# Values of a chunked gated recurrence on all four quarters of the TensorE array: odd heads' scores moved to the other half of the partitions, odd heads of v loaded there too

## The chip, the cores and the metric

The kernel runs on one core of one Trainium2 chip. The metric is the device time of one execution in microseconds (us), the median of several runs. The profile's span is the stretch from the first to the last recorded instruction of one execution. It lies about 2 us below that execution's time.

The engines carry short names: PE is TensorE's matmul, PEld its weight load, DVE VectorE, ACT ScalarE, POOL GpSimd, SP SyncE. A "q" behind a name means that engine's issuing of DMAs. L641 is line 641 of the kernel's file. The change adds lines, so one piece of code has two numbers:

| code | before | after |
|---|---|---|
| transposes of f, k, q | L535 | L541 |
| carried part (kept x qh) | L609 | L615 |
| scores | L619 | L626 |
| values | L641 | L649 |
| new state | L667 | L674 |
| first, second layer of the MLP | L711, L718 | L718, L725 |

## The reference, cut to what matters

```python
# q, k, v, f_logit: (batch 4, heads 8, seq 768, head_dim 48), fp32
f = 1.0 / (1.0 + np.exp(-f_logit))
for t in range(S):
    state = f[:, :, t, :, None] * state + np.einsum('bhd,bhe->bhde', k[:, :, t], v[:, :, t])
    y[:, :, t] = np.einsum('bhd,bhde->bhe', q[:, :, t], state)
x = y.transpose(0, 2, 1, 3).reshape(B, S, H * D)       # (4, 768, 384)
xn = (x - mean) / np.sqrt(var + 1e-06) * g_ln
out = x + np.maximum(xn @ w_ch1, 0.0) @ w_ch2          # 384 -> 1536 -> 384
```

## The kernel before

The 768 steps are cut into 12 chunks of 64. Within a chunk the recurrence becomes four small products per pair of batch and head: the carried part (old state times scaled q), the scores (scaled k times scaled q, 64 x 64, with a causal mask), the values (masked scores times v) and the new state (k transposed times v). The MLP follows for the rows of the chunk. The order of all pieces of work is a hand-written plan: chunk n+1's small products are placed between pieces of chunk n's MLP.

The 128 partitions are used as two halves of 64. A batch `b` of a pair of batches owns half `b`, and `r` is 0 for even heads and 1 for odd ones. A small product uses one quarter of the array: a row half (the partitions that its operands lie on) and a column half (the output partitions). In the values both halves are `b`:

```python
ps = two_banks(f"ps{n}").rearrange("s r (e t) -> s r e t", t=T)
for e in range(GA):                                   # 8 pairs of heads
    for b in range(2):
        for r in range(2):
            seg = 2 * e + b
            nc.tensor.matmul(ps[half(b), r, e], lhsT=kh[head_rows(r), seg],
                             rhs=qh[head_rows(r), seg], start=True, stop=True)
# ... sc = ps * causal (VectorE), kt = transposes of kh ...
for across_ in range(2):
    for e, (g, a) in enumerate(pairs):
        for b in range(2):
            r = b ^ across_
            nc.tensor.matmul(py[half(b), r, e * D:(e + 1) * D],
                             lhsT=sc[half(b), r, e], rhs=vt[half(b), g, 2 * a + r],
                             start=n == 0 and e == 0, stop=True, skip_group_check=True)
# ... x copied from py (ScalarE), statistics; then the new state:
for e, (g, a) in enumerate(pairs):
    for r in range(2):
        for b in range(2):
            nc.tensor.matmul(pn[half(r), b, e * D:(e + 1) * D], lhsT=kt[half(b), e, half(r)],
                             rhs=vt[half(b), g, 2 * a + r], start=True, stop=True)
```

The start of the plan is listed piece by piece. In it `l1f` loads f of chunk 1, `f`, `r` and `w` fetch, convert and write a piece of the weights, `a1.values` is a stage of chunk 1 and `m0` a piece of chunk 0's MLP:

```python
START = """
l0v f l0k l0q f l1k l1f a0.gates l1q a0.after a0.k_across a0.upto
a0.k f a0.q a0.scores r a0.causal l1v w a0.kt a0.values r a0.stats
w a1.gates a0.state a0.norm a0.turn m0 r a1.after f a1.k_across f a1.upto
...
"""
```

One count needs care. The code has 32 matmuls of values per chunk (8 x 2 x 2), so 384 in 12 chunks, and the trace has 768 records of them. Each of these fp32 matmuls shows as two records. "64 matmuls" in the prediction and "x64" in the profile are records.

## Time and profile before

| what | before | how to read it |
|---|---|---|
| median of the 3 runs | 523.44 us | 522.62 to 523.45 |
| span of the profiled run | 521.5 us | |
| TensorE busy | 95% of the span | with the chain of waits, 90% of which is PE: TensorE sets the time |
| values, busy | 24.8 us in 768 records | 32 ns a record, where the other small products take 18 to 19 ns |
| one chunk in steady state | 40.48 us | from a carried part to that of the next chunk |

The prediction shows and reads the lines of this profile.

### The profile page before, as it was taken

The numbers are of one execution on the slowest core, as the hardware profiler recorded it, in microseconds if no ns is written. First come the engines' busy times: TensorE is split into PE (matmuls) and PEld (weight loads), VectorE is DVE, ScalarE is ACT, GpSimd is POOL, SyncE is SP. The second block draws the span as 40 slices with busy tenths as digits, with TensorE's granted clock in tenths as the row PEclk, the third lists the DMA queues.
The fourth block names the chain that finished last, engine by engine and source line by source line (L and its number), as shares of the span: only waits on it lengthen the run. The fifth ranks groups of instructions, "written<-read, shape, count | busy, mean of one in ns | idle before, by whom it ended". The sixth has DMA issues, their size and how long they took to land.

```text
span 521.5 us, 10893 instructions
## 1 busy us (share of the span) xinstructions
PE 495.8 (95%) x4841; PEld 380.1 (73%) x4841; DVE 201.0 (39%) x286; ACT 129.6 (25%) x255; POOL 41.4 (8%) x53
## 2 busy tenths in 40 slices
PE   2789897999999999999999999999999999999996
PEld 1668774668867867877876876876876876886773
DVE  6789557534323432431521612603512522522000
ACT  3457672002202112112112211211211211221210
POOL 3215235000000000000000000000000000000000
PEclk9979999999999999999999999999999999999999
DMA  9976565513303303402501601600700610000001
GB/s 170 177 206 218 118 160 76 108 31 69 69 16 65 74 4 63 87 3 51 102 3 36 116 3 25 127 3 16 132 6 16 118 20 16 17 1 16 17 1 35
DMA packets 109703, 33.83 MB, mean 65 GB/s; under 512 B 102736, under 2 KB 105808, under 8 KB 109648
## 3 DMA queue, kind: packets, MB, share of 16 engines
q1 hardware_dynamic: 108192, 32.85, 30.8%
q8 instruction: 40, 0.66, 0.5%
q10 hardware_dynamic: 1456, 0.20, 0.2%
q14 instruction: 15, 0.12, 0.1%
HBM read 28.31 MB, written 4.72 MB: 63 GB/s over the span
## 4 chain that ended last, share of the span: by engine, by line
PE 90%; DVE 4%; DMA 2%; ACT 1%; POOL 1%; issue 1%; ACTq 0%; SPq 0%; DVEq 0%; POOLq 0%
PE ph L711 35%; PE po L718 35%; PE tr L535 6%; PE py L641 5%; PE ps L619 2%; PE py L609 2%; PE kp L632 2%; PE pn L667 2%; PE xp L696 2%; DMA kraw<-in_k_dram 1%; DVE w_0body L507 1%; DMA fraw<-in_f_logit_dram 1%; POOL w L511 1%; DVE w_0body L504 1%; DVE w_0upper L509 1%
## 5 line engine op out<-in xcount | busy, mean ns | idle before, releaser
L718 PE MATMUL po<-w,h 128*128 128x384 f32 x576 | 195.2, 492 | 3.9 <-POOL w L511 3.9
L711 PE MATMUL ph<-xt,w 128*128 128x256 f32 x864 | 196.2, 383 | 0.5 <-ACT xt L698 0.5
L711 PEld LDWEIGHTS ph<-xt,w 128*128 128x128 f32 x864 | 163.2, 192 | 24.5 <-issue 0.9
L718 PEld LDWEIGHTS po<-w,h 128*128 128x128 f32 x576 | 107.3, 191 | 72.8 <-POOL w L511 5.1
L713 ACT ACTIVATE h<-ph 128x512 f32<-128x512 f32 x72 | 42.8, 596 | 167.0 <-PE ph L711 167.0
L723 DVE TENSOR_TENSOR o<-x,po 128x384 f32<-128x384 f32 x24 | 13.3, 554 | 117.4 <-PE po L718 117.4
L549 DVE TENSOR_TENSOR_SCAN after<-gates,ends 128x1040 f32<-128x1040 f32 (+1 forms) x13 | 28.0, 2155 | 34.9 <-ACT gates L568 34.9
L698 ACT ACTIVATE xt<-xp,gain 128x128 f32<-128x128 f32 x72 | 20.1, 373 | 84.7 <-PE xp L696 84.7
L656 DVE BATCH_NORM_STATS2 stats<-x 128x6 f32<-128x384 f32 x24 | 13.0, 543 | 67.7 <-ACT x L652 67.7
L623 DVE TENSOR_TENSOR sc<-ps,causal 128x1024 f32<-128x1024 f32 x12 | 14.7, 1225 | 53.3 <-PE ps L619 53.3
L658 POOL TENSOR_SCALAR rstd<-mv 128x2 f32<-128x2 f32 x12 | 2.8, 235 | 378.4 <-DVE mv L657 378.3
L561 DVE TENSOR_TENSOR_SCAN upto<-gates,starts 128x1040 f32<-128x1040 f32 (+1 forms) x13 | 28.1, 2158 | 0.5
L641 PEld LDWEIGHTS py<-v,sc 64*64 64x64 f32 x768 | 23.3, 135 | 6.6 <-issue 5.5
L652 ACT COPY x<-py 128x384 f32<-128x384 f32 x24 | 10.3, 481 | 64.0 <-PE py L641 64.0
L641 PE MATMUL py<-v,sc 64*64 64x48 f32 x768 | 24.8, 219 | 0.7 <-DVE sc L623 0.7
L634 ACT COPY kt<-kp 128x512 f32<-128x512 f32 x24 | 12.9, 589 | 46.2 <-PE kp L632 46.2
L587 DVE TENSOR_TENSOR qh<-tr,upto 128x512 f32<-128x512 f32 x24 | 15.6, 686 | 20.8 <-PE tr L535 20.8
L535 PE MATMUL tr<-ident,fraw 128*128 128x128 f32 x96 | 13.8, 286 | 6.1 <-POOL gates L445 4.6
L511 POOL TENSOR_TENSOR w<-w_0upper,w_0units 128x768 int32<-128x768 int32 x7 | 15.3, 2190 | 35.7 <-DVE w_0upper L509 35.7
L535 PE MATMUL tr<-ident,kraw 128*128 128x128 f32 x96 | 13.7, 288 | 4.7 <-DMA kraw<-in_k_dram 4.5
L535 PEld LDWEIGHTS tr<-ident,fraw 128*128 128x128 f32 x96 | 11.6, 148 | 7.9 <-POOL gates L445 4.6
L587 DVE TENSOR_TENSOR kh<-tr,after 128x512 f32<-128x512 f32 x24 | 15.3, 677 | 5.1 <-PE tr L535 5.1
(88 smaller groups left out, 307.0 us busy)
## 6 DMA issues: line engine op xcount, KB each, us to landing
w_0words<-in_moe_w_ch_dram SPq DMA_DIRECT2D x7, 768.0 KB, 5.0
v<-in_v_dram SPq DMA_DIRECT2D x48, 96.0 KB, 3.0
kraw<-in_k_dram SPq DMA_DIRECT2D x48, 96.0 KB, 3.1
qraw<-in_q_dram SPq DMA_DIRECT2D x48, 96.0 KB, 3.1
out_dram<-o SPq DMA_DIRECT2D x48, 96.0 KB, 2.2
fraw<-in_f_logit_dram SPq DMA_DIRECT2D x46, 96.0 KB, 3.1
w_256words<-in_moe_w_ch_dram SPq DMA_DIRECT2D x1, 768.0 KB, 5.7
w_512words<-in_moe_w_ch_dram SPq DMA_DIRECT2D x1, 768.0 KB, 6.9
```

The source lines that it names most:

```text
L511: nc.gpsimd.tensor_tensor(out=to.bitcast(I32), in0=upper, in1=units, op=ALU.add)
L535: nc.tensor.transpose(pt[:, a * P:(a + 1) * P], src[:, g, 2 * a:2 * a + 2].rearrange("p h e -> p (h e)"), ident)
L549: nc.vector.tensor_tensor_scan(out=after.rearrange(flat)[:, c0:c1][:, ::-1], data0=gt[:, c0 + 1:c1 + 1][:, ::-1], data1=ends.rearrange(fla ...
L561: nc.vector.tensor_tensor_scan(out=upto.rearrange(flat)[:, c0:c1], data0=gt[:, c0:c1], data1=st.rearrange(flat)[:, c0:c1], initial=0.0, op ...
L587: nc.vector.tensor_tensor(out=dst[:, segs], in0=pt, in1=by[:, segs, 1:E1], op=ALU.mult)
L623: nc.vector.tensor_tensor(out=sc.rearrange("s r e t -> s (r e) t"), in0=ps.rearrange("s r e t -> s (r e) t"), in1=causal.unsqueeze(1).broa ...
L641: nc.tensor.matmul(py[half(b), r, e * D:(e + 1) * D], lhsT=sc[half(b), r, e], rhs=vt[half(b), g, 2 * a + r], start=n == 0 and e == 0, stop ...
L698: nc.scalar.mul(out=xt[:, m, g * P:(g + 1) * P], in_=pt[:, m], mul=gain[:, m:m + 1])
L711: nc.tensor.matmul(ph[:, j], lhsT=w1[:, m, (i + j) * P:(i + j + 1) * P], rhs=xt[:, m], start=m == 0, stop=m == KD - 1)
L713: nc.scalar.activation(out=h[:, i:i + 2], in_=ph, func=AF.Relu)
L718: nc.tensor.matmul(po, lhsT=h[:, i, g * P:(g + 1) * P], rhs=w2[:, i], start=i == 0, stop=i == KF - 1)
L723: nc.vector.tensor_tensor(out=o, in0=x[:, g], in1=po, op=ALU.add)
```

## The change

Its intent is that the values use all four quarters of the array in place of two. Scores of an odd head are written to the other partition half, `b ^ r`. The values of that head then read their scores and their v there, so its v must also lie there: four extra DMAs per chunk load the odd heads of v into a tile `vx` with the two halves exchanged. Three buffers are made single along the way, to pay for `vx` in memory.

```diff
-l0v f l0k l0q f l1k l1f a0.gates l1q a0.after a0.k_across a0.upto
-a0.k f a0.q a0.scores r a0.causal l1v w a0.kt a0.values r a0.stats
+l0v f l0k l0q l0x f l1k l1f a0.gates l1q a0.after a0.k_across a0.upto
+a0.k f a0.q a0.scores r a0.causal l1v l1x w a0.kt a0.values r a0.stats
 ...                                          # l{n}x likewise for all later chunks
+        if name == "x":
+            loaded[n, name] = raws.tile([P, G, NP, D], FP32, tag="rawx", name=f"vx{n}")
+            odd = v.rearrange("b (a r) s d -> b r s a d", r=2)
+            for b in range(B):
+                nc.sync.dma_start(out=loaded[n, name][(1 - b % 2) * T:(2 - b % 2) * T, b // 2],
+                                  in_=odd[b, 1, n * T:(n + 1) * T])
+            return
 ...
-        kh = work.tile([P, NS, T], FP32, tag="kh", bufs=2, name=f"kh{n}")    # qh, starts likewise
+        kh = work.tile([P, NS, T], FP32, tag="kh", name=f"kh{n}")
 ...
-                    nc.tensor.matmul(ps[half(b), r, e], lhsT=kh[head_rows(r), seg],
+                    nc.tensor.matmul(ps[half(b ^ r), r, e], lhsT=kh[head_rows(r), seg],
                                      rhs=qh[head_rows(r), seg], start=True, stop=True)
 ...
-        for across_ in range(2):
-            for e, (g, a) in enumerate(pairs):
-                for b in range(2):
-                    r = b ^ across_
-                    nc.tensor.matmul(py[half(b), r, e * D:(e + 1) * D],
-                                     lhsT=sc[half(b), r, e], rhs=vt[half(b), g, 2 * a + r], ...)
+        for e, (g, a) in enumerate(pairs):
+            for b in range(2):
+                for r in range(2):
+                    rows = half(b ^ r)
+                    nc.tensor.matmul(py[half(b), r, e * D:(e + 1) * D], lhsT=sc[rows, r, e],
+                                     rhs=vx[rows, g, a] if r else vt[rows, g, 2 * a], ...)
```

## The prediction

> **What bounds the kernel now.** I read the page's busy shares first, then the groups of TensorE instructions by shape, then the chain of waits in one steady unit (335 to 380 us), and last the timeline of the first 50 us. The page:
>
> ```profile
> PE 495.8 (95%) x4841; PEld 380.1 (73%) x4841; DVE 201.0 (39%) x286; ACT 129.6 (25%) x255; POOL 41.4 (8%) x53
> PE   2789897999999999999999999999999999999996
> DVE  6789557534323432431521612603512522522000
> PEclk9979999999999999999999999999999999999999
> DMA  9976565513303303402501601600700610000001
> PE 90%; DVE 4%; DMA 2%; ACT 1%; POOL 1%; issue 1%; ACTq 0%; SPq 0%; DVEq 0%; POOLq 0%
> ```
>
> TensorE (PE) is busy 95% of the 521.5 us span and carries 90% of the chain that ended last. Its gaps lie in the first seven slices of 13 us; after some 93 us it works without a break at full clock. There, a microsecond off TensorE is a microsecond off the kernel. In the first four slices DMA is busiest (9, 9, 7, 6 tenths), and there a transfer can matter.
>
> The four groups of small products, by shape (busy time, then mean ns of one):
>
> ```profile
> L641 PE MATMUL py<-v,sc 64*64 64x48 f32 x768 | 24.8, 219 | 0.7 <-DVE sc L623 0.7
> L619 PE MATMUL ps<-qh,kh 48*64 48x64 f32 x768 | 14.3, 226 | 0.0
> L667 PE MATMUL pn<-v,kt 64*64 64x48 f32 x704 | 13.2, 219 | 0.0
> L609 PE MATMUL py<-kept,qh 48*64 48x48 f32 x704 | 12.6, 220 | 0.0
> ```
>
> One instruction has the same latency in all four (219 to 226 ns), but the values (L641) take 24.8/768 = 32 ns of busy time each, and the others 18 to 19 ns. L641 pairs score rows of one half of the partitions with output partitions of the same half, so consecutive matmuls alternate between two quarters of the array; the others visit all four. The weight loads in a steady unit's timeline give the spacing without the tail:
>
> ```profile
> 341.61 1.02 PEld L609 LDWEIGHTS py<-kept,qh 48*64 48x64 f32 x64 [0.33 <-issue]
> 342.54 1.03 PEld L619 LDWEIGHTS ps<-qh,kh 48*64 48x64 f32 x64
> 349.82 1.89 PEld L641 LDWEIGHTS py<-v,sc 64*64 64x64 f32 x62 [0.55 <-issue]
> 351.67 1.03 PEld L667 LDWEIGHTS pn<-v,kt 64*64 64x64 f32 x62
> ```
>
> A single load lasts 0.135 us, so L609 starts one every (1.02-0.135)/63 = 14.0 ns, L619 every 14.2, L667 every (1.03-0.135)/61 = 14.7, and L641 every (1.89-0.135)/61 = 28.8 ns. That is almost exactly double. Each quarter comes round every 56 to 59 ns in all four groups, with 48 or 64 moving columns, with 48 or 64 rows. So I read the limit as one load-and-multiply per quarter per 57 ns.
>
> **What the Trainium skill says.** "TensorEngine Tiling (Array Packing)", section Tiling Modes, Key Properties: the 64x64 mode has four tiles that load and multiply independently, and changing the mode drains the engine. The 14 against 28.8 ns agree with independent quarters; the change keeps the mode. "TensorE: Matmul & The Clock Gate", Part 3, The mechanism: a weight load overlaps matmuls in flight only when its row group differs. The trace shows only sequences whose rows alternate, so it neither agrees nor disagrees; this is my main doubt, below. "PSUM — Partial Sum Buffer", PSUM bank collisions raise a hardware error: different column tiles may write one bank at once on disjoint partitions, different row tiles may not; the same section measured clashes of row tiles per bank and 32-partition quadrant. The new values write bank r from both row halves, though on different column halves; no such case is in this trace. The clock page's Part 1, the HAM clock gate: an idle array falls back to half clock. This trace agrees: after a sparse stretch, the 12 matmuls of L711 at 29.39 us take 5.46 us, and 2.59 us in steady state.
>
> **The change part by part.** (1) Scores of odd heads go to the other output half. L619 has the same 768 instructions, still rows 0,1,0,1, and the order of quarters becomes (0,0),(1,1),(0,1),(1,0) instead of (0,0),(1,0),(0,1),(1,1). Each is still used once in four: no change. The causal mask is the same on both halves, so VectorE's product (1225 ns each) stays.
>
> (2) The values run on four quarters. Per chunk 64 matmuls go from 28.8 to the others' 14.2 ns: 64 x 14.6 = 0.93 us. The steady chain says the same from another side: 1.93 us for 61 of the values against 1.08 us for the 64 of L609. The successors (L667, then L718) are TensorE work that is ready: the state product needs only v and kt, both long there. So the saving goes straight to the end for chunks 2 to 11: 10 x 0.93 = 9.3 us. In chunk 1 (values at 42.68 us) the chain also runs from scores through values to state and L711: another 0.9. Together 10.2 us.
>
> (3) Four more DMAs per chunk, 48 in all: 1024 packets of 192 B (48 x 4 bytes) per chunk. Queue 1 spends 30.8% of 521.5 us x 16 engines on 108192 packets, 23.8 ns each, so 1024 packets over 16 engines are 1.5 us, 18 us in all of largely idle engines. In steady state they are issued behind v (at 336 us in the unit above), two units ahead of use: free. In the start they are not:
>
> ```profile
> 12.38 0.62 SPq L482 DMA_DIRECT2D w_256words<-in_moe_w_ch_dram  x1
> 13.05 2.63 SPq L417 DMA_DIRECT2D kraw<-in_k_dram  x4
> 15.72 3.84 SPq L417 DMA_DIRECT2D fraw<-in_f_logit_dram  x4
> 19.61 3.80 SPq L417 DMA_DIRECT2D qraw<-in_q_dram  x4
> 19.52 2.07 PE L641 MATMUL py<-v,sc 64*64 64x48 f32 x64 [0.33 <-DVE sc L623]
> 22.34 1.37 PE L535 MATMUL tr<-ident,fraw 128*128 128x128 f32 x8 [0.75 <-PE py L641]
> ```
>
> SyncE's queue issues without a pause until 27 us, at 0.66 us a DMA or slower. The extra load of chunk 0 goes in at 12.38 us and pushes all behind it by about 2.7 us (four at 0.66). The last f load of chunk 1 goes out at 18.9 us and lands near 23.3, when the second half of the transposes at 22.34 starts (0.6 us of TensorE's wait is on this load). After the change it lands near 26. Transposes, state (1.1 us) and the first xp follow in TensorE's order; ScalarE's gates (1.07 us) then stand before the xt (0.88 each). Where L711 began at 29.39 us, I estimate 30.4. So chunk 0, which would have gained 0.9, instead loses about 1.0. The weight pieces come later too, but each is read well after landing (the third: issued 23.45, landing after 6.9 us, read at 35.38), and from the fourth on SyncE waits for stage buffers anyway (2.9 us on one).
>
> (4) kh, qh and starts have one buffer instead of two. The next chunk writes them after this chunk's scores and transposes, about 20 us earlier in the steady order: no wait. One 0.93 us memset goes from VectorE's start, where it then waits 2.06 us for ScalarE: nothing gained.
>
> Sum: -9.3 - 0.9 + 1.0 = -9.2 us, so 523.44 - 9.2 = 514.2. I put the point at 514.6, leaning slightly to the rivals that cost.
>
> **The rivals.** (a) Order within a row half. The new order is rows 0,1,1,0,0,1,1,0, so half of the matmuls follow one on the same row half. If a row half can begin a load only every 28 ns, as it does in every group now, and the issue of neighbours stays 14 ns apart, four matmuls take 28+14+28+14 = 84 ns, 21 ns each: the saving per chunk is 64 x 7.8 = 0.5 us, the total 11 x 0.5 - 1 = 4.5 us, the time 519. For it: the skill's sentence. Against it: a quarter's own period of 57 ns explains all four groups alone. I give it a quarter. A bank written from two row halves could cost in the same way; if it serialized them fully, nothing would be saved and the time would be about 524. I give that 7%.
>
> (b) The start hides everything or loses more. If the extra loads land in slack, chunk 0 gains too: -11.2, 512.3 us. If, instead, weight pieces arrive late (the fourth is read at 37.9 us and would land near 40, since the second extra load also sits ahead of it) and the clock stays low for longer, the start loses 3 us in place of 1: 516.5.
>
> (c) Another engine becomes the bound. VectorE is at 39%, ScalarE 25%, and the copies of py wait 64.0 us in all for TensorE, so they follow it. This is out in steady state.
>
> **Range and chances.** Full rate in the values (about 0.68) gives 512.3 to 516.5 according to the start; rival (a) gives 517 to 520. I take 512.2 to 519.5. The 2% line is 512.97 us, a gain of 10.5, which needs the full rate and a start that gains as well: 0.13. Slower by over 2% would need a stall that nothing here shows: 0.01.
>
> **What would show it.** In the changed profile L641's busy time should fall from 24.8 to about 13.5 us, the weight loads of one steady chunk from 1.89 to about 1.03 us, and L619 stay at 14.3. From one steady unit to the next (transposes of f at 325.94 and 366.43 us: 40.49 us) the period should become 39.56. The f transposes of chunk 1 should wait for DMA until some 26 us, and the first L711 begin near 30.4. I am wrong if loads of one row half queue up (spacing near 21 ns), if L619 slows in its new order, if the start costs over 3 us, or if VectorE waits for kh or qh to be read.

## The result, and the profile after

The changed kernel took 515.8 us (median of 4 runs, 514.72 to 516.4). The kernel before, on the same chip in the same rounds, took 523.03 us (4 runs, 520.26 to 523.45). The ratio is 0.9871, with a 95% interval of 0.9832 to 0.991, so the change is a small gain, within 2%. Here and below a ratio is the mean time of one kernel's fast runs over the mean time of the other's fast runs of the same rounds, so it is not quite the ratio of the medians that stand beside it.

The page of the changed kernel, in the same parts as the prediction shows them for the kernel before (busy time, three rows of the 40 slices, the chain of waits by engine):

```profile
PE 485.0 (94%) x4841; PEld 369.7 (72%) x4841; DVE 200.7 (39%) x285; ACT 129.8 (25%) x255; POOL 41.8 (8%) x53
PE   2698896999999999999999999999999999999995
PEclk9969999999999999999999999999999999999999
DMA  9977667433402502602601701700700610000001
PE 87%; DVE 5%; SPq 3%; issue 1%; ACT 1%; DMA 1%; POOL 1%; DVEq 0%; POOLq 0%
```

TensorE has the same 4841 instructions and is busy 10.8 us less (495.8 before). It is still the bound from the eighth slice on. Up to the eleventh slice the DMA row is one or two tenths higher here and there than before, SyncE's issuing has come into the chain (3%), and the granted clock of the third slice is 6 tenths, where before it was 7.

The groups of small products, by shape (busy time, mean ns of one, then idle time before them):

```profile
L649 PE MATMUL py<-v,sc 64*64 64x48 f32 x384 | 13.9, 220 | 1.7 <-issue 1.0 <-DVE sc L630 0.7
L649 PE MATMUL py<-vx,sc 64*64 64x48 f32 x384 | 13.9, 220 | 0.0
L626 PE MATMUL ps<-qh,kh 48*64 48x64 f32 x768 | 13.8, 219 | 0.1
L674 PE MATMUL pn<-v,kt 64*64 64x48 f32 x704 | 13.2, 226 | 0.0
```

The values are now two groups of half the size, one on v and one on vx. They run at the same time, so their two times of 13.9 us must not be added. Busy time over the whole span for that line alone comes from the view by windows (columns: window, its length, PE busy, PEld busy, clock, DMA share, GB/s):

```profile
0.00:513.70 513.70, 14.03 (x768) 12.42 (x768) 0.98 0.35 70
```

The values take 14.03 us, against 24.82 us by the same view before. One record still takes 220 ns. What fell is the spacing: 18 ns of busy time a record in place of 32. The chain of waits in one steady unit shows the same where it counts (start, length, engine, group, records):

```profile
341.68 1.08 PE py L609 x64
...
349.89 1.93 PE py L641 x61
```

```profile
336.14 1.08 PE py L615 x64
...
344.35 1.08 PE py L649 x64
345.43 0.93 PE pn L674 x64
```

The first fence is the kernel before and the second the changed one. The values' 1.93 us became the 1.08 us of the carried part, and the new state follows with no gap.

Where did the rest of the time go? The trace splits the run into three parts. "Start of chunk 2" is the first weight load of its carried part. The period is the mean over eight later chunks. The last VectorE instruction is the residual sum `o`, whose end marks the end of the computation. All times are in us:

| part | before | after | difference |
|---|---|---|---|
| start of chunk 2 | 100.94 | 100.92 | 0.0 |
| one steady chunk | 40.484 | 39.564 | -0.92 |
| end of the last sum `o` | 517.13 | 507.91 | -9.2 (ten chunks of 0.92) |
| from there to the end of the span | 4.4 | 5.8 | +1.4 |
| span | 521.5 | 513.7 | -7.8 |

So the steady part gained 9.2 us, the start gained nothing, and the end gave back 1.4 us.

**The start.** The timeline of the changed kernel (start, length, engine, instruction, count, and in brackets the idle time before it with what ended it):

```profile
12.29 2.61 SPq L415 DMA_DIRECT2D vx<-in_v_dram  x4
...
18.28 4.39 SPq L425 DMA_DIRECT2D fraw<-in_f_logit_dram  x4
...
24.28 2.14 PE L541 MATMUL tr<-ident,fraw 128*128 128x128 f32 x8 [3.80 <-DMA fraw<-in_f_logit_dram]
...
30.47 4.38 PE L718 MATMUL ph<-xt,w 128*128 128x256 f32 x12 [0.69 <-ACT xt L705]
...
34.68 1.04 PE L541 MATMUL tr<-ident,kraw 128*128 128x128 f32 x8
```

The first line is the extra load. It pushes the f load of chunk 1 from 15.72 us to 18.28 us, TensorE waits 3.80 us for it, and the first block of the MLP begins at 30.47 us, 1.1 us later than the 29.39 us of before. But that block takes 4.38 us where it took 5.46 us, so the transposes of k behind it begin at 34.68 us, where before they began at 34.64 us. The delay was gone again within one block. The view by windows says why: columns are window, length, PE busy, granted clock, DMA share and GB/s. The first line is the block in the kernel before, and the other two are the block in the changed kernel.

```profile
29.39:34.85 5.46, 5.46 (x13) 0.50 0.82 267
```

```profile
30.47:33.60 3.13, 3.13 (x8) 0.50 0.61 95
33.60:34.85 1.25, 1.25 (x8) 1.00 0.41 77
```

Before, the whole block ran at half of the clock. Here the full clock came back at 33.60 us, within the block, and 3.13/2 + 1.25 = 2.8 us at full clock is what 5.46/2 = 2.7 us is. So it is the clock that took the delay away. That it came back just then is not a gain to count on: in two more traces of the same kernel (r1, r3 below) it came back at 34.19 and 35.12 us, and the k transposes began at 34.98 and 35.43 us.

**Chunk 1.** Its values are at double rate as well, and no gain of it reaches the end of the start. The scores' mask on VectorE, the values and the normalization of x in the changed kernel:

```profile
41.28 1.23 DVE L630 TENSOR_TENSOR sc<-ps,causal 128x1024 f32<-128x1024 f32 x1 [0.47 <-PE ps L626]
...
44.67 0.25 PE L649 MATMUL py<-v,sc 64*64 64x48 f32 x1 [1.05 <-issue]
...
52.99 2.39 DVE L693 TENSOR_SCALAR xn<-x,mv,rstd 128x384 f32<-128x384 f32 x2
```

TensorE stops inside the values, after 57 of the 64 records, for about 1.1 us, and the profile shows nothing that it waited for ("issue"). That is about what the double rate saves there. Independently of it, VectorE is busy from the mask at 41.28 us to the end of this xn at 55.4 us (13.5 of 14.1 us), mostly with weight pieces. Before, the same two instructions began at 41.40 and 53.04 us.

**The end.** From the landing of the last output DMA to the end of the span the kernel before shows 1.60 us and the changed one 2.73 us. The page of the changed kernel lists 16 instruction fetches on queue 14, that of the kernel before 15; in the last 5 us there are four of these and three. I come back to this under the experiments.

### The profile page after: what moved, and what is told of

The parts are those of the page before. It is cut to its first block, busy times and chain, and to the rows that moved or that the text cites. A ratio compares the mean times of both kernels' runs of the same rounds, so it can differ in the third digit from the quotient of the medians.

```text
span 513.7 us, 10940 instructions
## 1 busy us (share of the span) xinstructions
PE 485.0 (94%) x4841; PEld 369.7 (72%) x4841; DVE 200.7 (39%) x285; ACT 129.8 (25%) x255; POOL 41.8 (8%) x53
## 4 chain that ended last, share of the span: by engine, by line
PE 87%; DVE 5%; SPq 3%; issue 1%; ACT 1%; DMA 1%; POOL 1%; DVEq 0%; POOLq 0%
PE po L725 35%; PE ph L718 34%; PE tr L541 6%; SPq L425 3%; PE py L615 2%; PE py L649 2%; PE pn L674 2%; PE ps L626 2%; PE kp L639 2%; PE xp L703 1%; DVE w_0body L514 1%; DMA fraw<-in_f_logit_dram 1%; POOL w L518 1%; DVE w_0body L511 1%; DVE w_0upper L516 1%
## 5 line engine op out<-in xcount | busy, mean ns | idle before, releaser
L649 PEld LDWEIGHTS py<-v,sc 64*64 64x64 f32 x384 | 12.3, 134 | 7.7 <-issue 6.6
L541 PEld LDWEIGHTS tr<-ident,kraw 128*128 128x128 f32 x96 | 11.7, 148 | 7.1 <-DMA kraw<-in_k_dram 5.3
```

The costliest lines, as they stand in the source:

```text
L541: nc.tensor.transpose(pt[:, a * P:(a + 1) * P], src[:, g, 2 * a:2 * a + 2].rearrange("p h e -> p (h e)"), ident)
L649: nc.tensor.matmul(py[half(b), r, e * D:(e + 1) * D], lhsT=sc[rows, r, e], rhs=vx[rows, g, a] if r else vt[rows, g, 2 * a], start=n == 0 a ...
```

## The experiments

The first question was whether the layout or the interleaving makes the gain, and whether the order of quarters matters. The second was what the start costs. The third was why chunk 1 gains nothing. Twelve runs were made, all with correct results. All edits are to the changed kernel.

### The changed kernel again, as a yardstick (r1, r3)

No edit.

> The changed kernel once more, unaltered, as the measure for the others and for what varies from run to run. Theory: the steady units give 9.2 us and the start gives nothing, because chunk 0 waits for the late f load (first L718 at 30.47 us) and chunk 1 is bound by VectorE from its masked scores to its normalized x (41.3 to 55.4 us). So the first product of chunk 2 (py<-kept) should again start near 101.0 us, as before the change, and the time stay at 515.2 plus or minus 1. The 1.05 us gap inside the values of chunk 1 (43.4 to 44.7 us) should come again if it is a property of the program. The 1.4 us longer tail after the last product should not come again if it is the chance of the last store. Rival: the tail belongs to the change, then the span is again 6.3 us longer than the end of the last product.

> The changed kernel once more, on the same chip: 515.5 plus or minus 0.7. Chunk 2 starts at 101.0 to 101.3 us where the transposes of kh in chunk 0 run at half clock or not; the stop after the 57th matmul of the values of chunk 1 comes again.

The first gave 515.54 us (514.19 to 516.2; ratio 0.9854, interval 0.9827 to 0.988) and the second 516.35 us (514.23 to 516.51; ratio 0.987, interval 0.9845 to 0.9896). With the first 515.8 us these are three medians of one kernel, 0.8 us apart, and its single runs spread over 2.3 us. A difference below a microsecond between two kernels is not shown by one such run. The three traces have the same steady period of 39.564 us, and chunk 2 starts at 100.92, 101.25 and 101.72 us, so the spread comes from the start.

The record also lists the granted clock of every run, and the time goes with it. In r3 the run of 514.23 us had 0.992 and the other four, 516.28 to 516.51 us, had 0.984 or 0.985. Of the runs of the kernel before that were made beside these experiments, ten at 0.990 to 0.993 took 521.63 to 522.51 us, and eleven at 0.987 or 0.988 took 522.78 to 524.96 us. So two kernels are best compared at like clocks. The gain of the change is not a matter of the clock: its four runs all had 0.985, less than any of these runs of the kernel before.

### The values of even and odd heads one after the other (e1)

```diff
-        for e, (g, a) in enumerate(pairs):
-            for b in range(2):
-                for r in range(2):
+        for r in range(2):
+            for e, (g, a) in enumerate(pairs):
+                for b in range(2):
```

Everything of the change stays: layout, extra loads, single buffers. Only the order within the values goes back to two quarters at a time.

> The changed kernel with the values in another order: all even heads first (quarters (0,0) and (1,1) in turn), then all odd heads (quarters (1,0) and (0,1) in turn). Same loads, same scores on the other half, same data. Theory (a quarter takes one load-and-multiply per 57 ns, and only the interleaving over four quarters pays): weight loads of a steady chunk every 28.8 ns again, period of a steady unit 40.49 us in place of 39.57, time about 9 us above the changed kernel, 524 to 525. Rival (the gain comes from what the change moves, such as odd heads read from their own tile on the other partitions): spacing near 14 ns and 515.

It took 522.14 us (521.74 to 523.13) against 522.24 us of the kernel before: ratio 0.9997, interval 0.997 to 1.0024. The gain is gone. That the time lies 1 or 2 us above the kernel before, as expected, did not come true; but the period below is a little shorter than before, so this does not show that the extra loads, the single buffers and the later end cost nothing: together they can have cost about the 1.8 us (ten periods of 0.18) that it saved. The chain in its steady unit:

```profile
347.52 1.64 PE py L649 x58
```

The first 26 weight loads of this unit take 0.84 us, so (0.84-0.135)/25 = 28.2 ns each, the old spacing. The period is 40.30 us, 0.18 us below that of before. In the trace of the unit the loads of the second pass begin at 348.19 us while those of the first still run until 348.46 us: at the hand-over of the passes, four quarters are in use for a moment, which would explain the 0.18 us. So the gain comes from having all four quarters in use together, and not from what the change moves.

### Two matmuls on one quarter in a row (e3)

```diff
-        for e, (g, a) in enumerate(pairs):
-            for b in range(2):
-                for r in range(2):
+        for e0 in range(0, GA, 2):
+            for b, r in ((0, 0), (0, 1), (1, 0), (1, 1)):
+                for e in (e0, e0 + 1):
+                    g, a = pairs[e]
```

All four quarters are in use, but each gets four records in a row before the next one follows.

> The changed kernel with the values two by two in the same quarter: (0,0) twice, (1,0) twice, (1,1) twice, (0,1) twice, for two values of e. All four quarters are still used equally. Theory A (matmuls start in order, and the second of a pair waits out its quarter's 57 ns): 28.5 ns a matmul, period about 40.5 us, 523 to 525 us. Theory B (TensorE's queue takes later work of a free quarter ahead): 14 to 15 ns, period 39.57 us, 515 us.

It took 515.33 us (two runs, 515.3 and 515.36; ratio 0.9861, interval 0.9828 to 0.9893), so the theory of strict order fell and that of work taken ahead held. The timeline of TensorE around the beginning of one block of values:

```profile
343.76 0.25 PE L650 MATMUL py<-v,sc 64*64 64x48 f32 x1
343.77 0.25 PE L650 MATMUL py<-vx,sc 64*64 64x48 f32 x1
343.79 0.25 PE L650 MATMUL py<-v,sc 64*64 64x48 f32 x1
343.80 0.25 PE L650 MATMUL py<-vx,sc 64*64 64x48 f32 x1
```

In the program the first vx record is the fifth, behind four on v that share one quarter. It started 10 ns after the first, ahead of three records that precede it. The period is 39.667 us, only 0.10 us more than that of the changed kernel. The same is in the trace of the kernel before, once one knows to look: records of the new state start at 351.61 us, and two of the values, which precede them in the program, at 351.67 us.

### Without the extra loads in the start (e4, e5)

```diff
# e5: chunk 0 without vx, values in the old way; e4: chunks 0 and 1
-l0v f l0k l0q l0x f l1k l1f a0.gates l1q a0.after a0.k_across a0.upto
+l0v f l0k l0q f l1k l1f a0.gates l1q a0.after a0.k_across a0.upto
-nc.tensor.matmul(ps[half(b ^ r), r, e], ...)
+nc.tensor.matmul(ps[half(b ^ r if n >= 1 else b), r, e], ...)       # e4: n >= 2
+if vx is None: ...the values loop of the kernel before...
```

> Chunk 0 in the old way and without its extra load, chunk 1 and all others in the new way: the f transposes of chunk 1 go back to 22.3 us and the first L718 to 29.4. Theory that VectorE holds chunk 1 whatever TensorE saves there: first product of chunk 2 at 101.0 us again, time as the changed kernel within 0.7 us. Rival (only the late f load ate the gain): chunk 1 then keeps its 0.9 us, first product of chunk 2 at 100.1 us, time 0.9 us below the changed kernel.

> Chunks 0 and 1 in the old way (two quarters, no extra load), chunks 2 to 11 in the new way. The start is then that of the kernel before: f transposes of chunk 1 at 22.3 us, first product of chunk 2 at 101.0 us. Theory (the start gains nothing in the changed kernel): same time as the changed kernel within 0.7 us. Rival 1 (the extra loads cost the start something hidden elsewhere, such as packets beside the weights): 1 to 2 us faster than the changed kernel. Rival 2 (the new values in chunks 0 and 1 do gain something): 1 to 2 us slower.

They took 516.08 us (515.36 to 516.32; ratio 0.9866, interval 0.9842 to 0.989) and 516.12 us (514.24 to 516.72; ratio 0.9861, interval 0.9837 to 0.9884), beside 515.54 us of the changed kernel in the same rounds (ratio 0.9854). Taking the loads away gains nothing, so they do not cost the start anything that shows in the time. In the traces chunk 2 starts at 101.50 (e5) and 102.28 us (e4), within and a little above what the changed kernel itself shows. One thing did not go as expected: the f transposes are back at 22.59 and 23.11 us, yet the first block of the MLP starts at 30.55 and 31.07 us and not at 29.4. There it waits for the normalization of chunk 0, whose values took 2.39 and 2.81 us on TensorE and began at 20.30 and 20.40 us (before: 2.09 us from 19.52 us). So an early f load alone does not bring that block forward.

### The f load ahead of the k load (e6)

```diff
-l0v f l0k l0q l0x f l1k l1f a0.gates ...
+l0v f l0k l0q l0x f l1f l1k a0.gates ...
```

> The changed kernel with the f load of chunk 1 issued before its k load in place of after it; k is not read until 34 us. Theory that the late f load costs the start: f transposes near 21.5 us instead of 24.28, clock not lowered there, first L718 near 28.6 us instead of 30.47, and if the rest follows the start is 1 to 2 us shorter, 513.5 to 514.5 us. Rival (VectorE and the weight loads hold the start whatever f does; the fourth weight piece lands at 39.1 us): first L718 earlier, first product of chunk 2 still at 101.0 us, time as the changed kernel.

It took 515.95 us (514.42 to 516.54; ratio 0.9857, interval 0.9831 to 0.9883), the same as the changed kernel. The wait itself did go: TensorE's wait for this f load is 0.31 us in place of 3.80 us. Yet the first block of the MLP starts at 30.18 us, 0.3 us earlier, and chunk 2 at 101.93 us. Removing 3.5 us of a wait in the start changed nothing at the end of it.

### The f load first and chunk 1's extra load later (e7, r2)

```diff
-l0v f l0k l0q l0x f l1k l1f a0.gates ...
-a0.k f a0.q a0.scores r a0.causal l1v l1x w ...
-w a1.gates a0.state a0.norm a0.turn m0 r a1.after f a1.k_across f a1.upto
+l0v f l0k l0q l0x f l1f l1k a0.gates ...
+a0.k f a0.q a0.scores r a0.causal l1v w ...
+w a1.gates a0.state a0.norm a0.turn m0 r a1.after f a1.k_across f l1x a1.upto
```

> As the run with f before k, and the extra load of chunk 1 issued after the fourth and fifth weight pieces in place of before them. These pieces then land 4 us earlier than in the changed kernel (the fourth by 35.5 us in place of 39.1). Theory that late weight pieces hold VectorE at 42.4 us: that work starts near 41.5 us and chunk 2 begins up to 0.9 us earlier than in the run with f first. Rival (VectorE is held by its own order from the masked scores of chunk 1 on): no change beyond 0.3 us at the same clock history.

> The reordered loads once more, for a comparison on one chip with the changed kernel: 514.2 against 515.5. If the two lie within 0.5 us, the earlier advantage was the chance of the start.

The first run of it gave 514.4 us (512.46 to 514.58; ratio 0.983, interval 0.9801 to 0.9859) and looked like a gain of about 1 us. The second, beside the changed kernel in the same rounds, gave 515.46 us (514.61 to 517.37; ratio 0.9873, interval 0.9848 to 0.9898) where the changed kernel had 0.987. The advantage was not reproduced. What does differ in both traces is that chunk 2 starts at 99.93 and 100.19 us, 0.7 to 1.8 us earlier than in the three traces of the changed kernel, and that TensorE stops for only 0.28 and 0.39 us within the values of chunk 1. The clock differs as well: all four runs of e7 had 0.991 or 0.992, the six of r2 0.982 to 0.991. I count it as not shown to be better.

### The normalization of chunk 1 ahead of a weight piece on VectorE (e9)

```diff
-f w w a1.stats r f a1.state m0 m0 r m0 w
-a1.norm l2k a1.turn w m0 m1 r f m1 m1 m1 w
+f w w a1.stats r f a1.state m0 m0 r m0
+a1.norm w l2k a1.turn w m1 m0 r f m1 m1 m1 w
```

The theory was that VectorE's order of work sets when chunk 1 is normalized, so that faster values have nothing to gain, and that moving the normalization would release it.

> The changed kernel with one thing reordered in the start: in chunk 1 VectorE makes the normalized x before it opens the sixth weight piece, and TensorE takes the first products of unit 1 before the last of unit 0, which need that piece. Theory that VectorE's order holds the start from 41 to 55 us in the changed kernel: xp starts 1.5 to 2 us earlier (53.5 in place of 55.5 us), the first product of chunk 2 starts near 99.6 in place of 101.0 us, time 1 to 1.5 us below the changed kernel. Rival (the opening of weights between 69 and 88 us holds the start whatever comes before): chunk 2 starts at 101.0 us again and the time is that of the changed kernel.

It took 516.62 us (514.12 to 517.05; ratio 0.9883, interval 0.9862 to 0.9904), so the expected 1 to 1.5 us did not come: a miss. The profiled run was its fastest by more than 1 us, 514.12 us, with chunk 2 at 99.57 us, so its trace does not stand for the others. It had a clock of 0.992, the other five 0.985 to 0.988, and it alone of all the traces has no second stretch at half clock. In that trace TensorE stopped for 2.6 us within the values of chunk 1, and its weight loads waited 1.7 us for ScalarE's xt until 56.05 us. The theory is neither shown nor refuted; in the times nothing of it is left.

### A pad of small matmuls in front (e10, e11)

```diff
+        if n == 0:
+            pad = two_banks("pad")
+            for i in range(16):
+                for b in range(2):
+                    for r in range(2):
+                        nc.tensor.matmul(pad[half(b), r, 0:16], lhsT=ident[half(r), half(r)],
+                                         rhs=ident[half(r), 0:16], start=True, stop=True)
```

This was for TensorE's stop in chunk 1. In eleven of the thirteen traces with the change it comes after the same instruction (record 471 of the weight loads, counted from the first), and a fetch of 16 KB of instructions lies within a microsecond or two of it. If the stop belongs to a place in the instruction stream, 64 matmuls ahead of it should move it along the program. e11 is the same pad in the kernel of e7.

> The changed kernel with 64 tiny matmuls (16 columns, result unused) put into TensorE's idle time before the k transposes of chunk 0 (6.5 to 11.8 us). They shift all later TensorE instructions by 128 places. In five of the traces so far TensorE stops for 0.7 to 2.6 us after exactly the same instruction, the 57th of the values of chunk 1, with nothing to wait for, and a 16 KB instruction fetch of its queue lies in that time. Theory (it runs out of fetched instructions at a block's edge): the stop moves 64 matmuls ahead, to the transposes of kh, and the values of chunk 1 run through without a gap. As VectorE's scores are waited for there anyway, the time falls by at most 1 us. Rival (the stop belongs to the values, such as the landing of their load): it stays after the 57th matmul.

> The reordered loads (f before k, the extra load of chunk 1 after two weight pieces) with the same 64 tiny matmuls. That reordering alone showed no stop in chunk 1, so I expect its time, 514, within 0.7 us; a gain of 1 us or more would say that something of the start still waits for instructions.

They took 516.14 us (514.16 to 517.45; ratio 0.9878, interval 0.9851 to 0.9904) and 516.18 us (513.45 to 518.55; ratio 0.9866, interval 0.9839 to 0.9892). The stop stayed at the very same place in the program (e10; the timeline of TensorE at the values of chunk 1):

```profile
45.51 0.25 PE L656 MATMUL py<-v,sc 64*64 64x48 f32 x1 [1.91 <-issue]
```

The seven records that are left of the values are the same, now after record 599 = 471 + 128. As I had written it, the expectation missed. But the test turned out not to separate the theories: the 64 matmuls of the pad showed as 128 matmul records and 128 loads, 256 instructions, which at 16 KB per fetch and 64 bytes per instruction is one whole fetch (the block size is the Trainium skill's, in "Runtime: NRT & Kernel Launch", section Instruction fetch mechanics; the traces show the 16 KB). A pad of one whole block moves every block boundary back onto the same instruction. A pad of another size would have decided it. In e11 the stop is 2.0 us, where e7 and its repetition had 0.28 and 0.39 us, and the 514 us expected of it did not come either.

The traces say more about the fetch than the pad did. In all eleven traces with a stop, TensorE's next weight load starts 1.20 to 1.57 us after the landing of the 16 KB fetch next to it (42.27 to 43.38 us in the changed kernel, next load at 44.67 us), although that landing lies anywhere from 41.5 to 46.3 us and the stop lasts 0.28 to 2.6 us. Where there is no stop, the same load comes 1.43 us (e6), 1.49 us (before) or 1.84 us (e4) after the landing. So the fetch is the likely cause of the stop; no run moved the fetch alone.

### All traces side by side

| kernel | median, us | start of chunk 2 | steady period | TensorE's stop in values of chunk 1 | last landing to end |
|---|---|---|---|---|---|
| before | 523.44 | 100.94 | 40.484 | none | 1.60 |
| changed | 515.8 | 100.92 | 39.564 | 1.17 | 2.73 |
| r1, changed | 515.54 | 101.25 | 39.564 | 0.66 | 2.62 |
| r3, changed | 516.35 | 101.72 | 39.564 | 0.65 | 2.62 |
| e1 | 522.14 | 99.67 | 40.300 | 1.68 | 3.03 |
| e3 | 515.33 | 99.78 | 39.667 | 2.61 | 2.95 |
| e4 | 516.12 | 102.28 | 39.564 | none | 2.91 |
| e5 | 516.08 | 101.50 | 39.565 | 0.56 | 2.90 |
| e6 | 515.95 | 101.93 | 39.564 | none | 3.00 |
| e7 | 514.4 | 99.93 | 39.564 | 0.28 | 3.10 |
| r2, as e7 | 515.46 | 100.19 | 39.564 | 0.39 | 2.72 |
| e9 | 516.62 | 99.57 | 39.564 | 2.58 | 3.02 |
| e10 | 516.14 | 100.95 | 39.564 | 2.04 | 2.95 |
| e11 | 516.18 | 103.97 | 39.564 | 2.03 | 2.89 |

(The stop is measured here between weight loads; the timeline's 1.05 us is between matmuls.) Three things stand out. The steady period is the same to the third digit wherever the values visit the four quarters in turn. The start of chunk 2 varies by 4 us and does not follow the stop: e3 and e9 have the longest stops and the earliest starts. And the end is 2.6 to 3.1 us in all thirteen traces of kernels with the change, against 1.60 us in the one trace of the kernel before.

What the start of chunk 2 does follow can be read from the same traces. Chunk 1's mask on VectorE starts 6.6 to 6.9 us after its k transposes in all fourteen, and chunk 2 starts 59.5 to 59.9 us after that mask in eleven of them: with the values of chunk 1 at either rate, and with stops of 0 to 2.0 us. The other three have their second stretch at half clock in another place (e3 60.9 us, e11 60.4 us) or have none (e9 59.7 us). So what TensorE saves or loses in the values of chunk 1 does not reach chunk 2. And the k transposes follow the first block of the MLP, which takes 2.83 us where it runs at full clock (e1, e3, e9, e10) and up to 5.46 us at half (before, e6, e11). Most of the spread is therefore made before chunk 1's k transposes, in good part by where the stretch at half clock falls. What places that stretch was not tested.

## Why the prediction was right or wrong

The time, 515.8 us, lies in the range and within 2%, 1.2 us above the point.

**Part 1, the scores' move is free: right.** Their busy time is 13.8 us (14.3 us before; other traces of the changed kernel have 14.4).

**Part 2, the values at the rate of the others: right for the steady chunks.** The period fell by 0.92 us where 0.93 us was predicted, and ten chunks gave 9.2 us where 9.3 us was predicted. The profile of the changed kernel shows it in the predicted places: busy time 14.03 us (13.5 predicted), a period of 39.564 us (39.56 predicted). The weight loads tell the spacing: in a steady unit of the changed kernel the first starts at 344.28 us and the 64th at 345.17 us, so 0.89/63 = 14.1 ns, in bursts of four every 58 ns. Experiment e1 shows that the interleaving is the cause, since without it the loads are 28.2 ns apart again and the time is that of before.

**Part 2, the other 0.9 us from chunk 1: wrong.** It was argued from the chain, in which scores, values, state and MLP follow one another. TensorE stopped there for about as long as the faster values saved, and VectorE was busy without a break until 55.4 us, before and after. The stop is not what hid the gain: e6 has none, and its time did not differ. From the mask of chunk 1 to chunk 2 it is 59.5 us in the kernel before and 59.6 to 59.7 us in the three traces of the changed one, so the faster values are not on the path that ends last there. That VectorE's order is that path is argued from its busy time and not shown: e9 changed the order, and its time did not improve.

**Part 3, the extra loads in the start cost 1.0 us: wrong in the sum, half right in the steps.** The f load was pushed by the predicted 2.6 us. It landed at 24.1 us, not at 26, and yet the first block of the MLP began at 30.47 us, as predicted (30.4), since the transposes and the state product then ran at a lower clock (2.14 us in place of 1.37 us, and 1.93 us in place of the 1.1 us reckoned with): two errors cancelled there. What failed is the step from there to "chunk 0 loses about 1.0". It took over the block's length from the kernel before; the block itself was 1.1 us shorter, as the full clock came back within it, and the next work began on time. e4 and e5 took the loads away and gained nothing. In the start, waits of TensorE mostly replace other waits: e6 took 3.5 us of one away, and nothing came of it.

**Part 4, single buffers are free: right.** Before kh VectorE waits for the transposes of k (4.0 us in all; 5.1 us before) and 0.6 us for its own work, never for a reader of the old kh, and the steady period fell by the whole amount of the values.

**The sum.** Two wrong terms of nearly the same size and opposite sign, -0.9 and +1.0 us, cancelled, by luck: the start as a whole was predicted at +0.1 us and measured at 0.0. (Even that is one trace against one: r1 and r3 start chunk 2 0.3 and 0.8 us later than the kernel before, and only one trace of that kernel was taken.) The error that remains is a term that was not in the sum at all: 1.4 us after the last sum of the output, of which 1.1 us lies after the last landing. Every one of the thirteen traces with the change has it, and the one trace of the kernel before has not. One instruction fetch more in the last 5 us goes with it in all thirteen (four in place of three), and the program is longer by 47 instructions (10940 against 10893). That the fetch is the cause is only argued; no run changed it alone, and one trace of the kernel before cannot say how much that end varies.

**The rivals.** Two sums at the edges of the range are slightly off (9.3 + 0.9 + 0.9 is 11.1 and not 11.2 us, and a start that loses 3 us gives 516.2 and not 516.5 us); nothing rests on them. Rival (a), that neighbours on one row half queue up, fell: it asked for 21 ns, and the changed kernel shows 14.1 ns with half of its neighbours on one row half. e3, with four records on one quarter in a row, shows why this order hardly matters: records for a free quarter start ahead of records that wait. The shared bank, written from both row halves into different partition halves, cost nothing either, and the results were correct. Rival (b), a start that gains or loses more, did not happen in the trace of the changed kernel, though the start of chunk 2 spreads over 4 us among all traces. Rival (c), another engine as the bound, did not happen.

## What to carry to other kernels

When small matmuls that use a quarter of the array take twice the time of others of the same shape, look at which quarters consecutive ones use: going round all four, in whatever order within a few instructions, was worth 0.92 us per chunk here, as much as the spacing of the weight loads had said. A gain read from a steady stretch can be multiplied by the number of stretches with confidence. A gain or cost read from a crowded start should not be added up term by term, as terms there replace one another and the granted clock moves them, and it needs several traces at like clocks, since three traces of one program already differed by 0.8 us.

## What the Trainium skill lacked or had wrong

- "TensorE: Matmul & The Clock Gate", Part 3, The mechanism, says that matmuls start and end in strict program order. Here they do not always start so: in e3 a record for a free quarter, the fifth in the program, started 10 ns after the first, ahead of three before it; in the kernel before, records of the new state started at 351.61 us, before values at 351.67 us that precede them.
- The same page, Part 1, the section on 56 against 53.3 ns, gives about 25 ns as the least time between the starts of two matmuls. It makes no exception there for tiles of the array, though its Part 3 has some 4 ns between the starts of packed tiles. Over four quarters the weight loads, and with them the matmuls, ran 14 to 15 ns apart on average here, in bursts of four that began 58 ns apart: in chunk 1 of the changed kernel four matmuls started between 42.65 and 42.67 us and the next four between 42.71 and 42.73 us. On two quarters the average was 28 to 29 ns.
- No page says that an fp32 matmul shows as two records, which matters for every count; the nearest is "FP8 and Floating Point Precision", TensorE Precision Notes, with four passes through the array for a true fp32 product. The 384 matmuls of the values showed as 768, the pad's 64 as 128, while the transposes (96 in the code for f) showed as one each.
- "Runtime: NRT & Kernel Launch", Instruction fetch mechanics, calls the fetching of instructions mostly hidden. Here TensorE stopped for 0.28 to 2.6 us in eleven of thirteen traces of changed kernels after the same instruction, and went on 1.20 to 1.57 us after the landing of a 16 KB fetch each time. That the fetch makes it stop is likely from this, but no run moved it alone.
